# Sum the half chunk of each early pair together with its other sums, and weigh two chunks at a time in the first batch

## The chip, the cores and the metric

One core of one Trainium2 chip. The time is the device time of one execution in microseconds; the kernel before has a median of 624.62 us over three runs (624.58 to 624.62). The names of the engines: PE is the matrix engine, DVE the vector engine, ACT the scalar engine, SP the engine that issues the loads.

## The reference, cut to what matters

Attention for 4 batches of 12 heads (448 queries and keys, 64 values a head), and behind it a two-layer network on the attention's output:

```python
scores = scale * np.matmul(q, k.transpose(0, 1, 3, 2))
scores = cap * np.tanh(scores / cap)
scores = scores - np.max(scores, axis=-1, keepdims=True)
attn = np.exp(scores)
attn = attn / (np.sum(attn, axis=-1, keepdims=True) + 1e-09)
out = np.matmul(attn, v)
h = x @ w_in                      # x: (1792, 768), w_in: (768, 2048)
g = np.where(pos, h, np.where(neg, 0.0, (h + beta) ** 2 / (4.0 * beta)))
y = g @ w_out                     # w_out: (2048, 768)
```

What the change touches is the sum over the keys and the product with v.

## The kernel before, in words

Two heads make a pair; pairs are numbered 0 to 23, six to a batch. Keys stand on the partitions, in four chunks: three of 128 keys, and a last one of 64 keys. In the last chunk both heads of the pair lie in one tile, head 0 on partitions 0 to 63 and head 1 on 64 to 127.

For a chunk c of pair n: `qk` (L362) makes the scores with three float16 products into one of two score tiles `s`; ACT takes the tanh (L370) and the exponential (L372) into a tile `e`; `av` multiplies it with the values `vt` into the one accumulator `av` (L436 for pairs 0 to 11, in float32; L424 for the later pairs, in float16 halves). DVE adds chunks 0 and 1 (L400), and for pairs 6 to 11 chunk 2 as well (L403), into a tile `sums`.

Sums over the partitions are products with a tile of ones into 32 columns, four of them side by side, one for each head and half of the queries, into the tile `t`. For pairs 0 to 11 (`n < HALVED`) the last chunk is summed right behind its own `av` step, with the 64 partitions of each head as they lie (L441); `norm` then adds the product of `sums` (L459), and for pairs 0 to 5 that of chunk 2 too (L459). DVE takes the reciprocal `rr` (L461), ACT or DVE rounds it into the high part of `mix` (L467), DVE makes the low part (L468), a product with `sel` spreads it over the partitions of the two heads (L472, called the spread below), and DVE multiplies the weighted values with it (L481) and splits the product in two float16 tiles `x` (L482, L483).

The network's first layer is L519 to L521, its second L548 to L550: long runs of float16 products, 128 by 128 by 448. Its weights come as 8-byte numbers; DVE turns each piece into two float16 parts in four or five steps (L274, L275, L276, L277 or ACT's L278, L279). DVE also splits queries and keys in two float16 parts (L347 on ACT or DVE, L348 on DVE, tile `spl`). The weights are handled in the first third of the run, while pairs 0 to 11 are computed.

No order is written by hand. Each step is given to a planner with an estimated cost and with the tiles that it reads and writes; the planner runs a list schedule forward and backward five times and takes the best, and each engine then gets its steps in that order. Every step's cost therefore acts on the order of all of them. In a step of `av` the planner counts 105 + 800 ns a chunk, in `norm` 500 + 400 ns for each further chunk.

`tsc` is the factor in front of the tanh (L577, L578); the first tanh waits for it. `qkr` is the tile in which queries and keys land; pair 0's comes in two loads, of 704 and of 256 columns, every other pair's in one of 960.

Of the kernel before, what the change touches and what calls it, by code (L numbers as in the profile page):

```python
# [17 lines left out]
P = 128  # L18
B, H, S, D = 4, 12, 448, 64
NPR = H // 2  # L20
NCK = 4
# [158 lines left out]
def fast_body(ctx, tc, flag, qkp, vp, cap, w_in, w_out, out):  # L180
# [12 lines left out]

    capb, capr, tsc, half = new("capb", [P, 1]), new("capr", [1, 1]), new("tsc", [P, 1]), new("half", [P, 1])
    row = new("row", [1, P])
    ones = new("ones", [P, 32])
    sel, low = new("sel", [P, 2, P], F32R), new("low", [P, 1])
    racc = new("racc", [P, B, 1])
    chk, chr_, okt = new("chk", [P, NCHK]), new("chr", [P, NCHK]), new("okt", [1, NCHK])
# [27 lines left out]
    def take(name, tiles):  # L227

        turn[name] = i = (turn.get(name, -1) + 1) % len(tiles)
        return tiles[i], [("%s%d" % (name, i), None)]  # L230
# [6 lines left out]
    def dve(n, fn, r, w, fast=False):  # L237
        either(r, w, dve_(n, fn, fast))

    def act(n, fn, r, w):  # L240
        either(r, w, act_(n, fn))
# [4 lines left out]
    def pe(cost, fn, r, w):  # L246
        either(r, w, ("PE", cost, fn))
# [142 lines left out]
    def direct(n):  # L390

        return 2 if n < NPR else 3 if n < HALVED else NCK
# [17 lines left out]
    def av(n, cs):  # L410
        if cs[0] == 0:
            st["av", n] = take("av", avs)
        (a, ak), (vt, vk) = st["av", n], st["vt", n]
        if n >= HALVED:
            vh, vk = st["vh", n]

            def run():
                for c in cs:
                    e = st["eh", n, c][0]
                    for x, y in ((0, 0), (0, 1), (1, 0)):  # L420
                        for j in range(2):
                            h = slice(j * D, (j + 1) * D)
                            w, m = (vh[:, x, j * 3 + c], e[:, y, j]) if c < 3 else (vh[h, x, 6], e[h, y, 0])
                            T.matmul(a[h, :S], lhsT=w, rhs=m, start=(c == x == y == 0), stop=(c == 3 and x == 1))  # L424
            pe(105 + 570 * len(cs), run, [k for c in cs for k in st["eh", n, c][1]] + vk + (ak if cs[0] else []), ak)
            return

        t, tk = st["t", n] = take("t", ts) if 3 in cs else (None, [])

        def run():  # L430
            for c in cs:
                e = st["e", n, c][0]
                for j in range(2):
                    h = slice(j * D, (j + 1) * D)
                    w, m = (vt[:, j * 3 + c], e[:, j]) if c < 3 else (vt[h, 6], e[h, 0])
                    T.matmul(a[h, :S], lhsT=w, rhs=m, start=(c == 0), stop=(c == 3))  # L436
                if c == 3:

                    for j, q, half in sums_at():
                        h = slice(j * D, (j + 1) * D)  # L440
                        T.matmul(t[q:q + 32, :S // 2], lhsT=ones[h], rhs=e[h, 0, half], start=True, stop=False, tile_position=(j * D, q))  # L441
        pe(105 + 800 * len(cs), run, [k for c in cs for k in st["e", n, c][1]] + vk + (ak if cs[0] else []) + ([("ones", None)] if tk else []), ak + tk)

    def sums_at():

        return [(j, (1 - j) * D + h * 32, slice(h * S // 2, (h + 1) * S // 2)) for j in range(2) for h in range(2)]

    def norm(n):


        (sm, mk), (a, ak), (t, tk) = st["sums", n], st["av", n], st["t", n] if n < HALVED else take("t", ts)
        (rr, rk), (xf, fk) = take("rr", rrs), take("xf", xfs)
        late = range(direct(n), 3)

        def run():
            for c in [None, *late]:
                for j, q, half in sums_at():
                    m = sm if c is None else st["e", n, c][0]
                    T.matmul(t[q:q + 32, :S // 2], lhsT=ones, rhs=m[:, j, half], start=(n >= HALVED), stop=(c == (late[-1] if late else None)), tile_position=(0, q))  # L459
        pe(500 + 400 * len(late), run, mk + [k for c in late for k in st["e", n, c][1]] + [("ones", None)] + (tk if n < HALVED else []), tk)  # L460
        dve(1340, lambda: V.reciprocal(rr, t[:, :S // 2]), tk, rk)  # L461
        act(S, lambda: A.copy(xf, a[:, :S]), ak, fk)


        (mix, mk) = take("mix", mixs)
        mh, ml = [(mk[0][0], 0)], [(mk[0][0], 1)]
        either(rk, mh, act_(S // 2, lambda: A.copy(mix[:, 0], rr)), dve_(S // 2, lambda: V.tensor_copy(mix[:, 0], rr), True))  # L467
        dve(S // 2, lambda: V.scalar_tensor_tensor(out=mix[:, 1], in0=mix[:, 0].bitcast(F32), scalar=low, in1=rr, op0=ALU.mult, op1=ALU.add), rk + mh + [("sel", None)], ml)  # L468

        def spread():  # L470
            for h in range(2):
                T.matmul(t[:, h * S // 2:(h + 1) * S // 2], lhsT=sel[:, h], rhs=mix[:, 1], start=(h == 0), stop=(h == 1), skip_group_check=True)  # L472
        pe(400, spread, ml + [("sel", None)], tk)
        x, xk = take("x", xs)
        st["x", n] = x, xk[0][0]
        xh, xl = [(xk[0][0], 0)], [(xk[0][0], 1)]
        scale = XS if n < HALVED else 1.0
        if n >= HALVED:
            for j, op in ((CS + n - HALVED, ALU.max), (CS + B * NPR + n - 2 * HALVED, ALU.min)):
                dve(S // 2, lambda j=j, op=op: V.tensor_reduce(out=chk[:, j:j + 1], in_=rr, op=op, axis=AX.X), rk, [("chk", j)])  # L480
        dve(S, lambda: V.scalar_tensor_tensor(out=xf, in0=xf, scalar=scale, in1=t[:, :S], op0=ALU.mult, op1=ALU.mult), tk + fk, fk)  # L481
        either(fk, xh, act_(S, lambda: A.copy(x[:, 0], xf)), dve_(S, lambda: V.tensor_copy(x[:, 0], xf), True))  # L482
        dve(S, lambda: V.tensor_tensor(out=x[:, 1], in0=xf, in1=x[:, 0], op=ALU.subtract), fk + xh, xl)  # L483

    def attention(n):

        split(n)
        if n >= HALVED:
            halve_v(n)
        if n + 2 < B * NPR:  # L490
            load_qk(n + 2)
        for c in range(NCK):
            if n < HALVED:
                qk(n, [c])
            elif c % 2 == 0:
                qk(n, [c, c + 1])
            expo(n, c)
            add(n, c)
            if n >= HALVED:
                halve(n, c)  # L500
            if n < NPR:
                av(n, [c])
            elif c % 2:
                av(n, [c - 1, c])
        if n + 2 < B * NPR:
            load_v(n + 2)
        norm(n)
# [61 lines left out]
            T.matmul(fs[1][:, :S], lhsT=x0[:, :P], rhs=x0, start=True, stop=True)  # L569
    pe(373 * WARM, warm, [("x%d" % (len(xs) - 1), 0)], [("f1", None)])  # L570
    dve(32, lambda: V.memset(ones, 1.0), [], [("ones", None)])
    act(1, lambda: A.activation(half, ones[:, :1], AF.Copy, scale=0.5 * math.sqrt(GS)), [("ones", None)], [("half", None)])
    dve(1, lambda: V.memset(lnes, math.log(ES)), [], [("tsc", 0)])
    dve(P, lambda: V.memset(row, 1.0), [], [("row", None)])
# [511 lines left out]
```

## Time and profile before

| what | value |
|---|---|
| median of 3 runs | 624.62 us |
| profiled execution, its own time | 624.7 us |
| its span | 622.9 us |
| PE busy | 610.5 us (98%) |
| DVE busy | 490.1 us (79%) |
| ACT busy | 402.1 us (65%) |

The span runs from the first to the last instruction. Ends of matmuls are modelled and overlap the next one's start, so the step from one start to the next start tells what a matmul costs. In the views of the time line a row is: start, duration, engine, line, operation, out<-in, shapes, count; what the engine waited for stands in brackets. A matmul in float32 stands as two records. Shapes of PE rows begin with rows*columns of the part of the array that is used: 128*64 is all rows and 64 columns.

### The profile page before, as it was taken

How to read it: one execution, taken by the hardware profiler on the slowest of the kernel's cores; microseconds unless marked ns; L12 is line 12 of the kernel's file. 1: busy time of each engine (PE TensorE's matmuls, PEld its weight loads, DVE VectorE, ACT ScalarE, POOL GpSimd, SP SyncE). 2: the span in 40 equal slices, each digit the busy share in tenths (PEclk: the TensorE clock that was granted, in tenths of full speed). 3: DMA queues.
4: the chain of work that ended last, by engine and by line, in shares of the span. 5: the costliest groups of instructions: out<-in, count | busy, mean ns of one | idle time of the engine just before them, and what ended most of it. 6: DMA issues, size and time to landing. Idle time of an engine off the chain costs nothing.

```text
span 622.9 us, 9197 instructions
## 1 busy us (share of the span) xinstructions
PE 610.5 (98%) x3686; PEld 285.6 (46%) x3686; DVE 490.1 (79%) x674; ACT 402.1 (65%) x587; POOL 0.9 (0%) x5
## 2 busy tenths in 40 slices
PE   7999999999999999999999999999999999999995
PEld 2233455433444444454454444444444555555552
DVE  6999999999999967998886669989975326667452
ACT  6999976899647658898754459989941015451000
POOL 0000000000000000000000000000000000000000
PEclk9999999999999999999999999999999999999999
DMA  8765525235364512423464342215134433337681
GB/s 326 278 237 190 163 69 202 79 119 193 110 250 157 173 41 66 129 65 103 134 207 168 129 149 83 86 63 155 61 133 166 150 128 105 98 93 248 217 290 38
DMA packets 25542, 91.13 MB, mean 146 GB/s; under 512 B 2834, under 2 KB 12178, under 8 KB 22418
## 3 DMA queue, kind: packets, MB, share of 16 engines
q1 hardware_dynamic: 25488, 90.45, 43.3%
q8 instruction: 31, 0.51, 0.3%
q14 instruction: 21, 0.17, 0.1%
q10 hardware_dynamic: 2, 0.00, 0.0%
HBM read 84.93 MB, written 5.51 MB: 145 GB/s over the span
## 4 chain that ended last, share of the span: by engine, by line
PE 82%; ACT 10%; DVE 4%; issue 1%; DMA 1%; SPq 0%; ACTq 0%; DVEq 0%
PE f L548 12%; PE f L549 11%; PE f L550 11%; PE f L519 10%; PE f L520 10%; PE f L521 10%; PE s L362 7%; PE av L424 4%; ACT e L372 4%; ACT e L370 4%; PE av L436 4%; PE t L459 2%; DMA qkr<-qkp 1%; PE t L472 1%; DVE z L381 1%
## 5 line engine op out<-in xcount | busy, mean ns | idle before, releaser
L519 PE MATMUL f<-x,w 128*128 128x448 f16 x384 | 135.6, 353 | 0.8 <-DVE wr L533 0.6
L548 PE MATMUL f<-g,w 128*128 128x448 f16 x384 | 135.5, 353 | 0.0
L549 PE MATMUL f<-g,w 128*128 128x448 f16 x384 | 135.4, 352 | 0.0
L550 PE MATMUL f<-g,w 128*128 128x448 f16 x384 | 135.3, 352 | 0.0
L521 PE MATMUL f<-x,w 128*128 128x448 f16 x384 | 135.3, 352 | 0.0
L520 PE MATMUL f<-x,w 128*128 128x448 f16 x384 | 135.3, 352 | 0.0
L370 ACT ACTIVATE e<-s,tsc 128x896 f32<-128x896 f32 (+1 forms) x96 | 86.0, 903 | 6.9 <-PE s L362 3.9
L290 DVE TENSOR_REDUCE chk<-raw 128x1 f32<-128x768 f32 (+1 forms) x56 | 58.2, 1060 | 23.2 <-DMA raw<-w_out 18.6
L555 ACT ACTIVATE ot<-f 128x448 f32<-128x448 f32 x24 | 13.0, 541 | 85.5 <-PE f L550 85.4
L362 PE MATMUL s<-spl 64*128 64x448 f16 (+1 forms) x504 | 67.0, 352 | 1.1 <-ACT e L370 1.0
L533 DVE SCALAR_TENSOR_TENSOR wr<-f,r 128x448 f32<-128x448 f32 x64 | 39.4, 616 | 26.5 <-ACT r L532 26.3
L531 ACT ACTIVATE r<-f,half 128x448 f32<-128x448 f32 x64 | 40.1, 627 | 24.7 <-PE f L521 24.6
L519 PEld LDWEIGHTS <-w 128*128 128x128 f16 x384 | 37.5, 98 | 39.7 <-issue 6.6
L548 PEld LDWEIGHTS <-w 128*128 128x128 f16 x384 | 37.5, 98 | 37.7 <-issue 4.0
L521 PEld LDWEIGHTS <-w 128*128 128x128 f16 x384 | 37.6, 98 | 35.0
L550 PEld LDWEIGHTS <-w 128*128 128x128 f16 x384 | 37.6, 98 | 34.9
L520 PEld LDWEIGHTS <-w 128*128 128x128 f16 x384 | 37.6, 98 | 34.4 <-issue 1.7
L549 PEld LDWEIGHTS <-w 128*128 128x128 f16 x384 | 37.6, 98 | 34.1 <-DVE w L279 0.5
L372 ACT ACTIVATE e<-e,lnes,capb 128x896 f32<-128x896 f32 (+1 forms) x48 | 49.3, 1038 | 0.9
L536 ACT ACTIVATE g<-wr 128x448 f16<-128x448 f32 x64 | 36.5, 571 | 20.5 <-DVE wr L533 20.4
L372 ACT ACTIVATE e<-e,capb 128x896 f32<-128x896 f32 (+1 forms) x48 | 45.4, 949 | 1.2
L436 PE MATMUL av<-e,vt 128*64 128x448 f32 (+1 forms) x192 | 44.1, 559 | 1.7 <-ACT e L372 1.6
(80 smaller groups left out, 732.4 us busy)
## 6 DMA issues: line engine op xcount, KB each, us to landing
qkr<-qkp SPq DMA_DIRECT2D x47, 480.0 KB, 3.7
raw<-w_out SPq DMA_DIRECT2D x17, 1024.0 KB, 4.8
raw<-w_in SPq DMA_DIRECT2D x18, 768.0 KB, 4.3
vt<-vp SPq DMA_DIRECT2D x48, 224.0 KB, 3.1
w<-w_in SPq DMA_DIRECT2D x14, 768.0 KB, 6.6
w<-w_out SPq DMA_DIRECT2D x7, 1024.0 KB, 5.0
out<-ot SPq DMA_DIRECT2D x24, 224.0 KB, 2.0
qkr<-qkp SPq DMA_DIRECT2D x1, 352.0 KB, 3.1
```

What stands on the lines that cost most here:

```text
L290: dve(width, lambda j=j, op=op: V.tensor_reduce(out=chk[:, j:j + 1], in_=hi, op=op, axis=AX.X, apply_absolute_value=True), rk + after, [(" ...
L362: T.matmul(s[:, j, :S], lhsT=t[h, a, S + c * P:S + (c + 1) * P], rhs=t[h, b, :S], start=(i == 0), stop=(i == 2))
L370: act(w * S + 60, lambda: A.activation(e[:, :w], s[:, :w, :S], AF.Tanh, scale=tsc), sk + [("tsc", None)], ek)
L372: act(w * S + 110, lambda: A.activation(e[:, :w], e[:, :w], AF.Exp, scale=capb, **bias), ek + [("tsc", None)], ek)
L436: T.matmul(a[h, :S], lhsT=w, rhs=m, start=(c == 0), stop=(c == 3))
L519: T.matmul(ph, lhsT=w1[:, 0, fc, c], rhs=x[c][0][:, 0], start=(c == 0), stop=False)
L520: T.matmul(ph, lhsT=w1[:, 1, fc, c], rhs=x[c][0][:, 0], start=False, stop=False)
L521: T.matmul(ph, lhsT=w1[:, 0, fc, c], rhs=x[c][0][:, 1], start=False, stop=(c == NCC - 1))
L531: act(S + (170 if acc else 0), lambda: A.activation(r, ph, AF.Relu, bias=half, scale=0.5 * root / (WS * XS), **acc), fk + [("half", None)] ...
L548: T.matmul(po, lhsT=hi[:, fc], rhs=gv[:, 0], start=(fc == 0), stop=False)
L549: T.matmul(po, lhsT=lo[:, fc], rhs=gv[:, 0], start=False, stop=False)
L550: T.matmul(po, lhsT=hi[:, fc], rhs=gv[:, 1], start=False, stop=(fc == NFC - 1))
```

## The change

- Pairs 0 to 11: the last chunk is no longer summed behind its `av` step. `norm` now sums it in the same run as `sums` and chunk 2, over all 128 partitions, with a new tile `halves` in place of ones: its first 32 columns are one on the first 64 partitions and zero on the others, its last 32 columns the other way round.
- Pairs 0 to 5: `av` takes chunks 0 and 1 in one step and 2 and 3 in one, as the later pairs did already.
- Three small fills of `halves` on DVE at the start.

```diff
-    ones = new("ones", [P, 32])
+    ones, halves = new("ones", [P, 32]), new("halves", [P, 2, 32])
...
-                if c == 3:
-
-                    for j, q, half in sums_at():
-                        h = slice(j * D, (j + 1) * D)
-                        T.matmul(t[q:q + 32, :S // 2], lhsT=ones[h], rhs=e[h, 0, half], start=True, stop=False, tile_position=(j * D, q))
...
-        late = range(direct(n), 3)
+        late = range(direct(n), NCK)
...
-                    T.matmul(t[q:q + 32, :S // 2], lhsT=ones, rhs=m[:, j, half], start=(n >= HALVED), stop=(c == (late[-1] if late else None)), tile_position=(0, q))
-        pe(500 + 400 * len(late), run, mk + [k for c in late for k in st["e", n, c][1]] + [("ones", None)] + (tk if n < HALVED else []), tk)
+                    w, m = (ones, m[:, j, half]) if c != 3 else (halves[:, j], m[:, 0, half])
+                    T.matmul(t[q:q + 32, :S // 2], lhsT=w, rhs=m, start=(c is None), stop=(c == (late[-1] if late else None)), tile_position=(0, q))
+        pe(500 + 400 * len(late), run, mk + [k for c in late for k in st["e", n, c][1]] + [("ones", None), ("halves", None)], tk)
...
-            if n < NPR:
-                av(n, [c])
-            elif c % 2:
+            if c % 2:
                 av(n, [c - 1, c])
...
+    dve(64, lambda: V.memset(halves, 0.0), [], [("halves", None)])
+    for j in range(2):
+        dve(32, lambda j=j: V.memset(halves[j * D:(j + 1) * D, j], 1.0), [], [("halves", None)])
```

Lines behind `av` have other numbers after the change: L436 is L435, L459 is L454, L461 is L456, L468 is L463, L472 is L467, L481 is L476, L483 is L478, L533 is L526, L537 is L530, L577 is L573. The number at the end of a name counts the tiles; `halves` makes it one higher for most.

PE, pair 0's last chunk and its sums, before:

```order
L362 MATMUL s_139<-spl_91 128x448
L436 MATMUL av_142<-e_97,vt_92 64x448 x2
L441 MATMUL t_143<-e_97,ones 32x224 x4
L459 MATMUL t_143<-sums_103,ones 32x224 x4
L459 MATMUL t_143<-e_96,ones 32x224 x4
L362 LDWEIGHTS spl_91
```

And after:

```order
L362 MATMUL s_140<-spl_92 128x448
L454 MATMUL t_144<-sums_104,ones 32x224 x4
L454 MATMUL t_144<-e_97,ones 32x224 x4
L454 MATMUL t_144<-e_98,halves 32x224 x4
L435 MATMUL av_143<-e_97,vt_93 64x448 x2
L435 MATMUL av_143<-e_98,vt_93 64x448 x2
L362 LDWEIGHTS spl_92
```

All three sums now stand in one run, ahead of the last two chunks' products with the values.

DVE at the start (the first pairs' splits and the factor of the tanh), before:

```order
L348 SCALAR_TENSOR_TENSOR spl_90<-qkr_88,spl_90 128x704
L348 SCALAR_TENSOR_TENSOR spl_90<-qkr_88,spl_90 128x256
L577 RECIPROCAL tsc<-t_143 128x1
L578 TENSOR_SCALAR tsc<-tsc 128x1
L579 TENSOR_SCALAR capb<-t_143 128x1
L348 SCALAR_TENSOR_TENSOR spl_91<-qkr_89,spl_91 128x960
L274 TENSOR_SCALAR z_86<-w_0_79 128x768
```

And after:

```order
L348 SCALAR_TENSOR_TENSOR spl_91<-qkr_89,spl_91 128x704
L348 SCALAR_TENSOR_TENSOR spl_91<-qkr_89,spl_91 128x256
L348 SCALAR_TENSOR_TENSOR spl_92<-qkr_90,spl_92 128x960
L573 RECIPROCAL tsc<-t_144 128x1
L574 TENSOR_SCALAR tsc<-tsc 128x1
L575 TENSOR_SCALAR capb<-t_144 128x1
L274 TENSOR_SCALAR z_87<-w_0_80 128x768
```

The factor of the tanh now stands behind pair 1's split. On ACT pair 0's 256 columns are split ahead of pair 1's 960 now (DVE did it before), and SP issues pair 1's load ahead of pair 0's 256 columns.

DVE ahead of pair 10's reciprocal (the last row), before:

```order
L348 SCALAR_TENSOR_TENSOR spl_91<-qkr_89,spl_91 128x960
L400 TENSOR_TENSOR sums_103<-e_94,e_95 128x896
L481 SCALAR_TENSOR_TENSOR xf_132<-xf_132,t_143 128x448
L483 TENSOR_TENSOR x_106<-xf_131,x_106 128x448
L403 TENSOR_TENSOR sums_103<-sums_103,e_96 128x896
L275 SCALAR_TENSOR_TENSOR z_86<-raw,z_86 128x1024
L533 SCALAR_TENSOR_TENSOR wr_135<-f_140,r_133 128x448
L276 SCALAR_TENSOR_TENSOR z_86<-raw,z_86 128x1024
L461 RECIPROCAL rr_129<-t_143 128x224
```

And after:

```order
L276 SCALAR_TENSOR_TENSOR z_87<-raw,z_87 128x1024
L275 SCALAR_TENSOR_TENSOR z_88<-w_5_85,z_88 128x1024
L478 TENSOR_TENSOR x_107<-xf_132,x_107 128x448
L276 SCALAR_TENSOR_TENSOR z_88<-w_5_85,z_88 128x1024
L400 TENSOR_TENSOR sums_104<-e_95,e_96 128x896
L476 SCALAR_TENSOR_TENSOR xf_133<-xf_133,t_144 128x448
L403 TENSOR_TENSOR sums_104<-sums_104,e_97 128x896
L526 SCALAR_TENSOR_TENSOR wr_137<-f_142,r_135 128x448
L296 TENSOR_REDUCE chk<-x_111 128x1
L348 SCALAR_TENSOR_TENSOR spl_91<-qkr_89,spl_91 128x960
L456 RECIPROCAL rr_130<-t_144 128x224
```

By this reciprocal one more piece of weights has gone through DVE after the change (the piece in `w_5` is under way, which before was begun behind it), and one more split.

## Rows read from the trace of the kernel before

**Rows 1.** Stretches of core 0: busy time and count of each engine.

```profile
18.00:61.80 43.80, 43.32 (x333) 14.63 (x331) 41.56 (x56) 42.33 (x56) 0.00 (x0) 1.00 0.64 232
61.80:115.00 53.20, 53.20 (x303) 25.88 (x300) 51.79 (x73) 43.13 (x68) 0.00 (x0) 1.00 0.39 129
115.00:162.50 47.50, 46.17 (x313) 16.47 (x310) 45.99 (x58) 46.72 (x67) 0.00 (x0) 1.00 0.40 133
```

**Rows 2.** What PE waited for, 0 to 163 us: total, times, longest.

```profile
PE av L436 <- ACT e L372: 1.6, 5, 0.4
PE t L472 <- DVE mix L468: 1.0, 2, 0.6
```

**Rows 3.** What DVE waited for, 0 to 163 us.

```profile
DVE rr L461 <- PE t L459: 2.1, 4, 1.1
DVE w L279 <- ACT w L278: 0.8, 2, 0.5
```

**Rows 4.** Time line of PE, pair 0's last chunk and its sums.

```profile
14.93 0.74 PE L362 MATMUL s<-spl 64*128 64x448 f16 x6
15.60 0.97 PE L436 MATMUL av<-e,vt 64*64 64x448 f32 x4
16.50 0.58 PE L441 MATMUL t<-e,ones 64*32 64x224 f32 x8
17.01 0.59 PE L459 MATMUL t<-sums,ones 128*32 128x224 f32 x8
17.41 0.56 PE L459 MATMUL t<-e,ones 128*32 128x224 f32 x8
17.91 0.74 PE L362 MATMUL s<-spl 64*128 64x448 f16 x6
```

**Rows 5.** Time line of PE: an av run of two chunks; one set of sums alone.

```profile
27.85 1.72 PE L436 MATMUL av<-e,vt 128*64 128x448 f32 x8
29.51 0.74 PE L362 MATMUL s<-spl 64*128 64x448 f16 x6
...
149.90 0.59 PE L459 MATMUL t<-sums,ones 128*32 128x224 f32 x8
150.42 1.60 PE L362 MATMUL s<-spl 64*128 64x448 f16 x9
```

**Rows 6.** Time line of DVE at the start.

```profile
6.80 0.17 DVE L577 RECIPROCAL tsc<-t 128x1 f32<-128x1 f32 x1 [0.92 <-PE t L576]
8.09 1.16 DVE L348 SCALAR_TENSOR_TENSOR spl<-qkr,spl 128x960 f16<-128x960 f32 x1 [0.86 <-ACT spl L347]
10.25 0.56 DVE L274 TENSOR_SCALAR z<-w 128x768 int32<-128x768 int32 x1 [1.00 <-DMA w<-w_in]
```

**Rows 7.** Time line of ACT at the start.

```profile
7.05 1.00 ACT L347 ACTIVATE spl<-qkr 128x960 f16<-128x960 f32 x1 [2.43 <-DMA qkr<-qkp]
7.96 0.99 ACT L370 ACTIVATE e<-s,tsc 128x896 f32<-128x896 f32 x1
```

**Rows 8.** Time line of DVE around the reciprocals of pairs 10 and 11.

```profile
150.64 1.55 DVE L461 RECIPROCAL rr<-t 128x224 f32<-128x224 f32 x1
...
158.29 0.69 DVE L274 TENSOR_SCALAR z<-w 128x1024 int32<-128x1024 int32 x1
158.89 1.55 DVE L461 RECIPROCAL rr<-t 128x224 f32<-128x224 f32 x1
160.35 0.56 DVE L537 SCALAR_TENSOR_TENSOR g<-wr,g 128x448 f16<-128x448 f32 x1
160.83 1.21 DVE L275 SCALAR_TENSOR_TENSOR z<-w,z 128x1024 int32<-128x1024 int32 x1
161.96 0.44 DVE L468 SCALAR_TENSOR_TENSOR mix<-mix,low,rr 128x224 fp32r<-128x224 f32 x1
```

**Rows 9.** Time line of PE: the spreads of pairs 10 and 11, and the last products.

```profile
154.01 0.48 PE L472 MATMUL t<-mix,sel 128*128 128x224 f32 x2 [0.34 <-DVE mix L468]
162.46 0.48 PE L472 MATMUL t<-mix,sel 128*128 128x224 f32 x2 [0.61 <-DVE mix L468]
...
616.13 0.35 PE L549 MATMUL f<-g,w 128*128 128x448 f16 x1
616.32 0.35 PE L550 MATMUL f<-g,w 128*128 128x448 f16 x1
```

More of the change, by code (lines that the diff above doesn't have):

```diff
@@ L426, in av @@
             return
-        t, tk = st["t", n] = take("t", ts) if 3 in cs else (None, [])
         def run():
@@ L436, in run @@
                     T.matmul(a[h, :S], lhsT=w, rhs=m, start=(c == 0), stop=(c == 3))
-                if c == 3:
-                    for j, q, half in sums_at():
-                        h = slice(j * D, (j + 1) * D)
-                        T.matmul(t[q:q + 32, :S // 2], lhsT=ones[h], rhs=e[h, 0, half], start=True, stop=False, tile_position=(j * D, q))
-        pe(105 + 800 * len(cs), run, [k for c in cs for k in st["e", n, c][1]] + vk + (ak if cs[0] else []) + ([("ones", None)] if tk else []), ak + tk)
+        pe(105 + 800 * len(cs), run, [k for c in cs for k in st["e", n, c][1]] + vk + (ak if cs[0] else []), ak)
     def sums_at():
@@ L448, in norm @@
     def norm(n):
-        (sm, mk), (a, ak), (t, tk) = st["sums", n], st["av", n], st["t", n] if n < HALVED else take("t", ts)
+        (sm, mk), (a, ak), (t, tk) = st["sums", n], st["av", n], take("t", ts)
         (rr, rk), (xf, fk) = take("rr", rrs), take("xf", xfs)
-        late = range(direct(n), 3)
+        late = range(direct(n), NCK)
         def run():
```

## The prediction

> **What bounds the kernel now.** I read the stretches first, then the waits of PE and DVE, then the time line where they meet. In the stretches from 18 to 162.5 us, where pairs 0 to 11 are computed and the weights are taken apart, the reader should see that no engine has room: PE is busy for 142.7 of 144.5 us, DVE for 139.3, ACT for 132.2 [rows 1]. A busy PE alone would not say that PE is the bound, but the waits do: it waited for ACT 1.6 us in five places and for DVE 1.0 us at two spreads [rows 2]. So PE leads here, and DVE follows with 5.2 us of idle time. Part of that idle time is PE's doing: four reciprocals waited 2.1 us for the sums [rows 3]. At pair 11 DVE is the late one already: its reciprocal starts at 158.89, though PE was done with the sums, and the spread behind it keeps PE waiting until 162.46 [rows 8, 9]. From there PE runs nearly without a gap to its last product at 616.32 [rows 9].
>
> **The change part by part.** *PE, the sums.* Each change of the array's shape costs PE time, and that is what the change removes. One set of sums alone takes 0.52 us (149.90 to 150.42), two sets in a row 0.90 (17.01 to 17.91), so one more set of the same shape costs 0.38 [rows 4, 5]. The old set of the last chunk, in a shape of its own, took 0.51 (16.50 to 17.01) [rows 4]. Moved, it costs 0.13 less, and in twelve pairs that is 1.6 us. The zeros in `halves` cost nothing that these rows show: both shapes stream 224 columns for four products side by side.
>
> The Trainium skill (TensorEngine Tiling (Array Packing), Restrictions and Gotchas, Gotcha 1) says that different row tiles must not use one PSUM bank at the same time. The old sums do just that, two heads on different rows into `t`; by that rule they would have run one head after the other, some 0.8 us a set, and the change would give back about 4 us more. The trace does not agree: 0.51 us for the whole set [rows 4].
>
> *PE, two chunks a step.* One chunk of `av` takes 0.90 us up to the next shape (15.60 to 16.50), two take 1.66 (27.85 to 29.51), so a merged step saves 0.15 and the scores around it about 0.1 more [rows 4, 5]. But the planner had merged many of them already: along PE's order the runs of full chunks fall from 25 to 23 only. All in all PE's order has 255 changes of shape before and 241 after. At the 0.10 to 0.15 us that each pair of neighbours costs on the time line, they come to 25.0 and 22.4 us: 2.6 us less, 2.3 of it ahead of pair 11's spread and 0.3 behind. If PE alone set the time, this would be the gain.
>
> *The start.* The order puts the factor of the tanh behind pair 1's split on DVE. Before it was ready at about 7.2 us and the first tanh started at 7.96, when ACT was through with pair 1's split [rows 6, 7]. After, ACT has 256 columns more in front (at 1.00 us for 960, about 0.3 us) and starts pair 1's split when that load has landed, between 6.2 and 7.05 us; it ends at 7.4 to 8.3. DVE's low part takes 1.16 more, the factor 0.4, so the first tanh starts at 9.0 to 9.9: 1.0 to 1.9 us late. I take 1.5. The trace of before can't show how much of it stays. Its cover is DVE: DVE starts on the weights when their load lands, at 10.25, both times [rows 6], and by pair 5 ACT has about 1.7 us less to do, since the order gives some of it to later pairs. So I take nothing for it as long as DVE sets the time, and 1.5 if that cover is gone.
>
> The Trainium skill (TensorE: Matmul & The Clock Gate, the table at its beginning) calls DVE's and ACT's queues strictly first in, first out, with eight entries. That speaks against this change: the factor can't overtake the split. The trace agrees as far as it goes, since all of DVE's instructions start in the program's order; if they could overtake, the 1.5 us would be nothing.
>
> *DVE, ahead of pairs 10 and 11.* The change takes nothing off DVE, but the new order moves work forward. Counted along the order, pair 10's reciprocal has ahead of it, more than before: one step each of L274, L275, L276 and L279 on 1024 columns (0.60 and three times 1.13 from start to start), a split in both parts (1.07 and 0.57), and two steps of 0.53, less a rounding of 0.30 that ACT takes: 6.4 us [rows 8]. The split's low part is the 1.16 of the start less 0.09 by which DVE's rows overlap [rows 6]; the last ones are estimated from rows of the same width. Pair 11's reciprocal has the same 6.4 us ahead of it.
>
> **The sum.** It is made at pair 11's spread, since PE has all attention of pairs 0 to 11 ahead of it in both orders. Behind it PE has less to do after the change: 1971 products of the network instead of 1995, at 0.19 us each (616.13 to 616.32) 4.55 us, and 0.3 for fewer shapes; 4.85 in all. So the end moves by (new spread - 162.46 - 4.85) [rows 9]. Say DVE saves s us of its idle time on the way.
>
> By DVE: pair 11's reciprocal comes at 158.89 + 6.4 - s. From it to the spread it was 3.57 us with L537 and L275 between; L274 stands there too now, 0.60, so 4.2 [rows 8, 9]. The spread comes at 169.5 - s.
>
> By PE: pair 10's reciprocal comes at 150.64 + 6.4 - s, its spread 3.5 us later (3.37 before, and a copy of 0.15) [rows 8, 9]. From that spread to the next PE has pair 11's first step of `av`, six products of the network, two sets of sums, the second step of `av` and 21 products, with their changes of shape 9.9 us at the prices above. The spread comes at 170.4 - s.
>
> The later of the two counts: 170.4 - s, and the end moves by 3.1 - s. For s, zero is one end; the other is about 4.6, all of DVE's 5.2 us but what it waits for ACT (0.8 of it at L279 [rows 3]). I take 2.6: the 2.1 us in which reciprocals waited for PE go, since DVE is now the one behind, and 0.5 of the rest. That gives +0.5 us. The profiled execution took 624.7 us, 0.08 more than the median; on the median that is 625.1 us. So the 2.6 us that PE saves turn into waits at the spreads of pairs 6 to 11. This last part of the forecast has its own range, 623.4 to 625.9.
>
> **The rivals.** *PE keeps the lead.* If DVE runs with hardly any idle time (s of 4.4 or more), PE's savings come through: up to 2.6 us, 622.0. For it: DVE has 5.2 us to give. Against it: DVE, ACT and PE all hang on each other here, and a chain of three full engines does not run without gaps. With s at 4.4 it begins to count as faster, 623.4.
>
> *DVE keeps its idle time.* The same 6.4 us of weights and splits stand ahead of pair 10's reciprocal, but DVE still waits for loads, roundings on ACT and exponentials as before (s under 1.8). PE then stands at the spreads of pairs 10 and 11 for 3 to 5 us in all, and the end moves by +1.3 to +3.1: 625.9 to 627.7. For it: PE waited for these two spreads before [rows 2, 9]. Against it: part of the idle time was PE's doing.
>
> *The start stays.* ACT, which is 97% busy from 18 to 61.8 us [rows 1], never wins back the late tanh; then reciprocals of pairs 2 to 5 come 1.5 us late, DVE waits for them, and the end moves by 0.5 + 1.5 = 2.0 us: 626.6. Against it: the 1.7 us that ACT has less to do by pair 5.
>
> **How the numbers follow.** The forecast, no change that can be told, has 0.42. PE keeps the lead: 0.24. DVE keeps its idle time: 0.24. The start stays: 0.10. A change under 0.2% (1.25 us) can't be told from none here, so faster is 0.24, same 0.42, slower 0.34. The stretch behind pair 11, where the planner has moved work too, adds about 1 us either way, which no row here settles. Left out below is the end of the faster case and above that of the slowest, a tenth each: 622.4 to 627.6.
>
> **What would show it.** In the profile after: no PE row with 64*32; three sets of sums in a row, 1.27 us up to the next shape; the first tanh at 9.0 to 9.9 us; PE waiting for DVE at L467 for 3 us or more between 60 and 170 us, against 1.0 before; pair 11's spread at about 167.8. If that spread starts before 166 us with PE's waits no longer than before, DVE was not the bound and the forecast is wrong on the fast side; if PE waits over 5 us there, on the slow side. If the first tanh stands at 8 us, my reading of the start is wrong.

## The result, and the profile after

The changed kernel takes 627.0 us (median of eight runs, 626.35 to 631.21), the kernel before 624.62 (eight runs beside them): a ratio of 1.0052, 95% interval 1.0037 to 1.0066. It is slower by 2.4 us, where I forecast no change (625.1). The profiled execution took 627.01 us, its span is 625.1. Single runs are longer the lower the granted clock: 626.35 at a mean of 0.999, 631.21 at 0.992.

The stretches that answer to [rows 1], with the start ahead of them (us; busy time and count of PE, PEld, DVE, ACT, POOL; PE's granted clock; DMA share; GB/s):

```profile
9.00:12.00 3.00, 1.39 (x9) 0.51 (x8) 2.46 (x4) 2.93 (x4) 0.00 (x0) 0.99 1.02 418
12.00:15.30 3.30, 3.30 (x11) 0.88 (x12) 3.30 (x6) 3.23 (x5) 0.00 (x0) 0.50 1.01 419
...
18.00:61.80 43.80, 43.59 (x339) 15.65 (x337) 43.34 (x59) 41.49 (x57) 0.00 (x0) 1.00 0.67 242
61.80:115.00 53.20, 51.34 (x291) 24.85 (x288) 52.22 (x74) 42.13 (x65) 0.00 (x0) 1.00 0.35 118
115.00:162.50 47.50, 46.71 (x317) 17.48 (x318) 44.44 (x55) 46.20 (x64) 0.00 (x0) 1.00 0.46 161
```

Two stretches are new. PE is busy for 1.39 of 3.00 us from 9 to 12 us (2.39 before, at a clock of 1.00 there and behind it), and then works at half its clock. And from 61.8 to 115 us, where it was busy all of 53.20 us before, it has 1.9 us of idle time.

What PE waited for, up to 163 us (answers to [rows 2]):

```profile
PE s L362 <- ACT e L370: 4.5, 4, 1.9
PE f L562 <- DVE x L558: 2.0, 1, 2.0
PE t L467 <- DVE mix L463: 0.7, 1, 0.7
PE f L512 <- DVE wr L526: 0.5, 1, 0.5
```

The waits at the spreads (L467), which I had put at 3 us or more, are 0.7. In their place PE waits 4.5 us at the scores until the tanh has read the score tile out, 3.1 of it at the start. (L562 is the warm-up, outside the forecast.) That kind of wait was there before as well, in one place, a row that the prediction left out when it read PE's waits for ACT:

```profile
PE s L362 <- ACT e L370: 1.0, 1, 1.0
```

DVE's waits for the sums have gone from 2.1 to 0.9, in the direction forecast, but a wait for exponentials has come (answers to [rows 3]):

```profile
DVE sums L400 <- ACT e L372: 2.0, 2, 1.3
...
DVE rr L456 <- PE t L454: 0.9, 2, 0.6
```

Behind 163 us, PE's one wait, before and after:

```profile
PE f L519 <- DVE wr L533: 0.6, 2, 0.3
```

```profile
PE f L512 <- DVE wr L526: 2.2, 3, 1.0
```

The start, on the time line (answers to [rows 4, 6, 7]):

```profile
5.46 1.31 ACT L347 ACTIVATE spl<-qkr 128x256 f16<-128x256 f32 x2 [0.87 <-DMA qkr<-qkp]
...
6.80 1.16 DVE L348 SCALAR_TENSOR_TENSOR spl<-qkr,spl 128x960 f16<-128x960 f32 x1 [0.47 <-ACT spl L347]
7.88 0.16 DVE L573 RECIPROCAL tsc<-t 128x1 f32<-128x1 f32 x1
8.32 1.01 ACT L370 ACTIVATE e<-s,tsc 128x896 f32<-128x896 f32 x1 [1.56 <-DVE capb L575]
9.38 0.74 PE L362 MATMUL s<-spl 64*128 64x448 f16 x6 [1.86 <-ACT e L370]
...
11.35 0.73 PE L362 MATMUL s<-spl 128*128 128x448 f16 x3 [1.22 <-ACT e L370]
...
12.01 3.26 PE L435 MATMUL av<-e,vt 128*64 128x448 f32 x8
...
16.50 0.59 PE L454 MATMUL t<-sums,ones 128*32 128x224 f32 x8
...
16.90 0.56 PE L454 MATMUL t<-e,ones 128*32 128x224 f32 x8
...
17.28 0.56 PE L454 MATMUL t<-e,halves 128*32 128x224 f32 x8
```

The factor stands behind pair 1's split, and ACT waits 1.56 us for it and the bound computed with it; PE then waits twice for ACT. The weighted values at 12.01 took 3.26 us at half the clock; the same group took 1.72 in [rows 5]. The sums' last set is in the new shape.

The reciprocals and spreads of pairs 10 and 11 and the last product (answer to [rows 8, 9]):

```profile
154.27 1.55 DVE L456 RECIPROCAL rr<-t 128x224 f32<-128x224 f32 x1
...
164.07 1.55 DVE L456 RECIPROCAL rr<-t 128x224 f32<-128x224 f32 x1
```

```profile
158.64 0.37 PE L467 MATMUL t<-mix,sel 128*128 128x224 f32 x1
...
168.44 0.35 PE L543 MATMUL f<-g,w 128*128 128x448 f16 x1
168.47 0.43 PE L467 MATMUL t<-mix,sel 128*128 128x224 f32 x1
...
618.74 0.35 PE L543 MATMUL f<-g,w 128*128 128x448 f16 x1
```

The last product starts 2.42 us later than before. By the sum's own rule the spread accounts for 168.47 - 162.46 - 4.85 = 1.16 of it; the stretch behind the spread, 450.27 us instead of the 449.01 that the rule expects (453.86 before, less 4.85), for 1.26.

### The profile page after: what moved, and what is told of

Same layout as the page of the kernel before. It is cut to its first block, busy times and chain, and to the rows that moved or that the text cites. A ratio compares the mean times of both kernels' runs of the same rounds, so it can differ in the third digit from the quotient of the medians.

```text
span 625.1 us, 9185 instructions
## 1 busy us (share of the span) xinstructions
PE 608.9 (97%) x3686; PEld 287.0 (46%) x3686; DVE 490.0 (78%) x676; ACT 401.3 (64%) x588; POOL 0.9 (0%) x5
## 4 chain that ended last, share of the span: by engine, by line
PE 70%; ACT 16%; DVE 11%; issue 2%; DMA 1%; SPq 0%; ACTq 0%; DVEq 0%
PE f L541 12%; PE f L542 11%; PE f L543 11%; PE f L512 7%; PE f L513 6%; PE f L514 6%; PE s L362 6%; ACT e L370 5%; ACT e L372 5%; PE av L424 4%; PE av L435 4%; PE t L454 2%; DVE wr L526 2%; ACT r L525 1%; DVE g L530 1%
## 5 line engine op out<-in xcount | busy, mean ns | idle before, releaser
L526 DVE SCALAR_TENSOR_TENSOR wr<-f,r 128x448 f32<-128x448 f32 x64 | 39.8, 621 | 19.5 <-ACT r L525 18.9
L530 DVE SCALAR_TENSOR_TENSOR g<-wr,g 128x448 f16<-128x448 f32 x64 | 39.4, 619 | 6.6 <-ACT g L529 5.7
```

Source lines behind the costliest of these rows:

```text
L526: dve(S, lambda: V.scalar_tensor_tensor(out=w, in0=ph, scalar=WS * XS, in1=r, op0=ALU.max, op1=ALU.min), fk + rk, wk)
L530: dve(S, lambda: V.scalar_tensor_tensor(out=t[:, 1], in0=w, scalar=down, in1=t[:, 0], op0=ALU.mult, op1=ALU.subtract), wk + [(gk, 0)], [(g ...
```

## The experiments

Each is timed beside the kernel before, on one chip; the chips differ from run to run. The starts (us) of the spreads of pairs 0, 5, 6, 11 and of the last product in each profile locate a gain, where two kernels have one order:

| kernel | median us | ratio to before, 95% | spread 0 | 5 | 6 | 11 | last product |
|---|---|---|---|---|---|---|---|
| before | 624.6 | 1 | 21.73 | 65.49 | 114.30 | 162.46 | 616.32 |
| changed | 627.0 | 1.0052 [1.0037, 1.0066] | 20.90 | 62.26 | 113.52 | 168.47 | 618.74 |
| e1 | 624.1 | 0.9987 [0.9978, 0.9996] | 21.46 | 64.93 | 113.61 | 161.75 | 615.59 |
| e6 | 628.09 | 1.0050 [1.0037, 1.0063] | 20.85 | 62.75 | 114.12 | 169.20 | 619.48 |
| e8 | 623.67 | 0.9983 [0.9974, 0.9992] | 22.79 | 64.86 | 109.70 | 167.33 | 615.25 |
| e10 | 623.66 | 0.9989 [0.9981, 0.9998] | 22.72 | 64.65 | 109.38 | 166.88 | 614.91 |
| e4 | 627.06 | 1.0046 [1.0029, 1.0063] | 20.21 | 61.58 | 112.83 | 167.76 | 618.02 |
| e5 | 627.15 | 1.0039 [1.0026, 1.0052] | 20.52 | 61.91 | 113.16 | 168.12 | 618.40 |
| e14 | 626.97 | 1.0031 [1.0020, 1.0043] | 21.44 | 62.80 | 114.05 | 169.03 | 620.03 |
| e15 | 627.04 | 1.0034 [1.0024, 1.0045] | 20.38 | 61.74 | 113.00 | 167.96 | 618.25 |
| e16 | 624.33 | 0.9998 [0.9989, 1.0007] | 21.37 | 65.10 | 113.91 | 161.75 | 615.59 |
| e17 | 626.44 | 1.0031 [1.0019, 1.0044] | 21.20 | 62.56 | 113.07 | 167.79 | 618.09 |
| e18 | 626.29 | 1.0024 [1.0013, 1.0035] | 20.86 | 62.23 | 112.75 | 167.47 | 617.77 |
| e19 | 626.15 | 1.0029 [1.0016, 1.0042] | 20.20 | 61.30 | 112.56 | 167.51 | 617.78 |

e1, e16 have before's order; e10 has e8's; e4 to e6 and e14 to e19 (but e16) have the changed kernel's, but for the steps moved or added.

Each place comes from one profile, and two things scatter in it. The first tanh starts at 8.22 to 8.88 us in the eight profiles of the changed order with nothing moved ahead of it, so the places carry some tenths of a us of the start; differences between two places of one profile don't. And a profiled run's time is 8.0 to 9.7 us more than the start of its last product, from kernel to kernel without a pattern, so medians of few runs are coarser than the places.

### What the new shape is worth by itself

e1: the kernel before, its order kept; only the last chunk's sums take the new shape.

```diff
-            for c in [None, *late]:
+            for c in [None, *late, *([3] if n < HALVED else [])]:
...
+                    w, m = (ones, m[:, j, half]) if c != 3 else (halves[:, j], m[:, 0, half])
```

> The order of all engines is the kernel before's, step for step; only the last chunk of pairs 0 to 11 is summed with the masked ones, in one run with the other sums, and the masked ones are filled in the step that fills the ones. So the shapes of the array change 12 times less (243 changes instead of 255) and nothing else moves. Theory A (PE leads in that order, and what the change lost it lost by the new order): PE gives back 0.13 us a pair, 1.6 us in all, and the time falls to about 623.0 us (622.8 to 623.6). Theory B (PE, ACT and DVE are all full in this stretch, so PE's savings drown in waits whatever the order): 624.2 to 624.8 us, with PE waiting 1 to 1.6 us more for ACT and DVE between 14 and 163 us.

e6: the changed kernel, its order kept; those sums in their old shape.

```diff
-                    w, m = (ones, m[:, j, half]) if c != 3 else (halves[:, j], m[:, 0, half])
+                    h = slice(j * D, (j + 1) * D)
+                    w, m = (ones, m[:, j, half]) if c != 3 else (ones[h], m[h, 0, half])
...
-        ... tile_position=(0, q))
+        ... tile_position=(0 if c != 3 else j * D, q))
```

> The changed kernel's order word for word, but the last chunk's sums in their old shape (64 rows of ones per head, 64*32), at their new place behind the other sets. 254 runs of one shape on PE instead of 242. If PE leads in this order too, the old shape costs 12 x 0.13 = 1.6 us: 628.6. If PE waits anyway (the theory: the saving is eaten by about 1 us of waits), 0.6 us: 627.6. If PE's savings are worth nothing in this order: 627.0.

In before's order the new shape brings the last product 0.73 us forward, in the changed order 0.74 (619.48 - 618.74); counted from PE's first score it is 0.68 and 0.84. e1's interval lies below 1, while e6's and the changed kernel's overlap. Neither time fell into a range that I had given: e1's 624.10 lies between Theory A and Theory B, e6's 628.09 between the counts with 0.6 and with 1.6 us. So the shape is a gain of about 0.7 us, less than half of the 12 x 0.13 = 1.6 that I counted. And e6, which has the old shape, still ends 619.48 - 616.32 = 3.2 us behind the kernel before (2.3 to 3.9 by the interval of its times): that is what the new order costs, with the sums' new place and the steps of two chunks in it, and that is the case.

### What other orders bring

e8: the kernel before, only the planner told of the set's cost. e10: e8's order with e1's shape.

```diff
-        pe(105 + 800 * len(cs), run, ...
+        pe(105 + 800 * len(cs) + (400 if tk else 0), run, ...
```

> The kernel before, instruction for instruction, with one number of the planner changed: the step with the last chunk of pairs 0 to 11 is given 400 ns more, for the sums that it holds and that the planner did not count. Only the order moves. Theory A (the order is what costs; a planner that counts PE's sums packs the other engines' work differently, and a new order is worth one or two us either way): a time clearly apart from 624.6, by my guess slower, 625.5 to 628. Theory B (an order that counts rightly is better): 622.5 to 624. Theory C (orders of this planner are all alike): 624.3 to 625.0.

> The order of the kernel before as the planner makes it when it counts 400 ns for the last chunk's sums (623.67 us by itself), with those sums in the new shape (64*32 becomes 128*32, no shape of their own). Theory (a new order moves the time through short waits, and the shape's saving is partly eaten by waits, 0.6 us in the order of the kernel before): about 623.0 us, between 622.4 and 623.5. Rival (PE's saving comes through in full, 12 x 0.13): 622.1. Rival (any saving of PE's turns into waits): 623.7.

e9 and e13: the changed kernel's steps, the planner counting 0 or 200 ns for the last chunk's set in place of 400.

```diff
-        pe(500 + 400 * len(late), run, mk ...
+        pe(500 + 400 * (len(late) - (n < HALVED)), run, mk ...              # e9
+        pe(500 + 400 * len(late) - (200 if n < HALVED else 0), run, mk ...  # e13
```

> The changed kernel with all its steps; only the planner's cost of the step with the sums leaves the last chunk's set out (100 + 400 per other set less, as the kernel before had it), so that only the order is another. Theory (it is the order that the planner found which costs 2.4 us, by waits at the start, at 62 to 92 us and behind pair 11): another order has other waits, between 624 and 627 us, and the waits of PE for the tanh at 62.9 us need not be there. Rival (the steps cost by themselves: two chunks at a time come late, three sets in a row hold PE up): 627 again.

> The changed kernel, the planner counting 200 ns instead of 400 for the last chunk's set; same steps, another order (the changed kernel 627.0 with 400, 625.04 with 0). Theory (each order is a draw, the price has no trend): anywhere from 623.5 to 627.5. Rival (counting the set pushes work behind it smoothly): midway, 626.0.

e2 is the first part alone, e3 the second; e12 is e10 with the second part.

```diff
-            if c % 2:                  # e2, against the changed kernel
+            if n < NPR:
+                av(n, [c])
+            elif c % 2:
...
-            if n < NPR:                # e3 against before, e12 against e10
-                av(n, [c])
-            elif c % 2:
+            if c % 2:
```

> The first part alone: sums of the last chunk in the new shape and place, weighted values chunk by chunk as before, the planner's own order. 251 runs of one shape on PE instead of 256 before and 242 after. If the sums' part carries the cost: 626 to 627 us. If the steps of two chunks carry it: 624 or less. Theory (the order found each time decides, not a part): either, with waits of PE in other places than after's 62.9 us.

> The second part alone: the first batch's weighted values in steps of two chunks, the last chunk's sums in their old shape and place, the planner's own order. 255 runs of one shape on PE, one less than before. Theory (the order found decides, not a part): within 1.5 us of the kernel before, 623.0 to 626, and the difference is PE's idle time, as its places in the profile show. Rival (steps of two chunks make PE wait for the second chunk's exponential): 626 or more, with PE waiting at L435.

> Both parts of the change's idea without moving the sums in the planner's list: sums of the last chunk in the new shape, but t taken and 400 ns counted in the step of the weighted values as in the faster order (623.66 us without this edit), and that step of two chunks. A new order once more. Theory (the order decides): between 622.5 and 626, its distance from 623.66 equal to the difference in PE's idle time and shape changes. Rival (two chunks a step save 0.1 to 0.25 us each and are always a gain): 623.0 or less.

A number that changes no instruction moved the kernel before to 623.67 us (e8, faster, against what I expected) and the changed kernel to 625.04 (e9, 1.0010 [0.9998, 1.0022]) and 624.53 (e13, 1.0001 [0.9993, 1.0010]). Prices of 0, 200 and 400 ns give 625.0, 624.5 and 627.0: no trend, so the rival of a smooth push falls. e2 came to 626.54 (1.0036 [1.0023, 1.0049]), e3 to 625.11 (1.0017 [1.0002, 1.0032]), e12 to 627.03 (1.0052 [1.0033, 1.0071]). e2's time is the one that I had named for the case that the sums' part carries the cost. But e13 has both parts, step for step as the changed kernel, and stands level with before, so the steps don't force the loss: the order does. Two chunks a step are not always a gain either: the same edit on e10 cost 3.4 us, more than either side of that forecast allowed. e10 adds next to nothing to e8 (last product 0.34 us earlier, medians alike), as the last rival there had it.

### What in this order costs: the start

e4 puts pair 0's first chunk of weighted values, for which all is ready, into PE's wait; e5 puts 13 products there whose result nobody reads, and e11 does so in e9.

```diff
+            if n == 0 and cs == [2]:             # e4, in the step of the scores
+                st["early"]()                    # av of chunk 0, taken out of the step [0, 1]
...
+            if n == 0 and cs[0] in (1, 2):       # e5, e11
+                for _ in range((0, 8, 5)[cs[0]]):
+                    T.matmul(fs[1][:, :S], lhsT=x0[:, :P], rhs=x0, start=True, stop=True)
```

> The changed kernel in its own order, with one thing undone: pair 0's first chunk is multiplied with its values right behind the scores of chunk 2, as in the kernel before, and no longer together with chunk 1. Theory A (the wait at the start starves PE, its clock falls to 1.2 GHz for some us, and this is what scatters the changed kernel's times): the granted clock stays at full from the first score on, PE's step with chunks 0 and 1 no longer takes 3.2 us, the runs lie within 1 us of each other, and the median falls by 0.5 to 1.5 us, to 625.5 to 626.5. What is left over the kernel before (1 to 1.8 us) is the order behind. Theory B (the start explains everything): 624.6 or below. Theory C (the scatter has another cause): runs from 626.3 to over 629 as before.

> The changed kernel in its own order, with 13 more products of zeros on PE in the two gaps of the start (8 behind the scores of chunk 1, 5 behind those of chunk 2, into a bank that nothing uses yet): PE does more and is idle less, and nothing else moves. Theory A (idle PE lets the clock fall): no stretch at half clock before the end, the scatter goes, the median is that of the changed kernel's undisturbed runs, 626.3 to 626.7 us. Theory C (the clock falls for another reason): the scatter stays, 626.3 to 631 us.

> The changed kernel with the order found when the planner leaves the last chunk's set out of its cost (625.04 us, single runs from 623.4 to 627.6 with a granted clock from 0.997 down to 0.992), and 13 products of zero's value to nobody (8 and 5) in PE's two waits for the first tanhs, as in the changed kernel with a filled start. Theory (PE's waits at the start let the granted clock fall in part of the runs, and that is the scatter): runs within 1 us of each other, about 624.0. Rival (the scatter comes from the waits at 60 to 66 us, where this order's profile shows the clock at half level from 64.6 to 68.0): scatter as before, 625.0.

The medians stayed at 627, against the forecasts of a gain. e4's runs scatter as before (626.44 to 629.90), though its one profile shows no fall of the clock at the start. But e5's five runs lie within 626.58 to 627.46, where the changed kernel's go to 631.21, and so do those of e15 and e18 below, which have the same filling (626.45 to 627.50 and 625.50 to 627.44). So filling the start takes the long runs away; the median it hardly moves. e11 took away e9's longest runs (623.77 to 626.36 instead of 623.39 to 627.63) but not a group some 2 us above the lowest, and its median is 625.16 (1.0009 [0.9999, 1.0019]), the rival's. e9's profile shows the fall at 64.6 us:

```profile
56.00:64.60 8.60, 6.98 (x62) 3.14 (x61) 8.38 (x12) 7.42 (x11) 0.00 (x0) 1.00 0.53 173
64.60:68.00 3.40, 3.40 (x11) 0.79 (x9) 3.26 (x6) 3.40 (x5) 0.00 (x0) 0.50 0.18 33
```

In e5 spread 0 came 0.38 us earlier, and spreads 5, 6, 11 and the last product 0.35, 0.36, 0.35 and 0.34: the order is rigid, and what the start gives is kept to the last product. The 0.38 is not an earlier tanh's doing, for e5's came 0.21 us later. From the first tanh to spread 0 it takes 12.0 us in the profiles of e4, e5, e15 and e18, and 12.6 in those of the changed kernel, e14 and e17, in which the clock fell at the start: such a fall costs 0.6 us. So e19 takes away what the forecast named there. Three steps on DVE are moved in the finished order:

```diff
+        todo, k = plan.order(), st["tsc"]        # k, k + 1, k + 2: factor and bound, L573 to L575
+        p = [j for j, (i, e) in enumerate(todo) if e == "DVE" and todo.index((k, "DVE")) > j][-1]
+        moved = [x for x in todo if x[0] in (k, k + 1, k + 2)]
+        todo = [x for x in todo[:p] if x not in moved] + moved + [x for x in todo[p:] if x not in moved]
```

> The changed kernel's order with three steps of VectorE moved by hand: the factor of the tanh and the bound (L573 to L575) ahead of the low part of pair 1's split, which stands in front of them in this order and behind them in the kernel before. Nothing else moves. The first tanh starts at about 7.0 us instead of 8.32. Theory (in this order the start is on the path: with the filled start every later spread and the last product stood 0.34 to 0.38 us earlier, as the first spread did): spread 0, spread 11 and the last product 0.7 to 1.3 us earlier, median 625.7 to 626.3. Rival (a later wait takes the gain, as with the moved scores): 627.

```profile
6.66 0.17 DVE L574 RECIPROCAL tsc<-t 128x1 f32<-128x1 f32 x1 [0.38 <-PE t L572]
...
7.34 1.01 ACT L370 ACTIVATE e<-s,tsc 128x896 f32<-128x896 f32 x1 [0.63 <-PE s L362]
8.40 0.74 PE L362 MATMUL s<-spl 64*128 64x448 f16 x6 [0.53 <-ACT e L370]
```

The first tanh starts at 7.34 instead of 8.32; spread 0 stands 0.70 us earlier, spread 5, spread 11 and the last product all 0.96. The median is 626.15, the lowest run 625.33 against 626.35. These are the theory's numbers, but they are not the factor's alone. The clock did not fall in e19's profile and did in the changed kernel's; against e4 and e5, where it did not fall either, e19's last product is only 0.24 and 0.62 us earlier, and PE now waits 0.95 us for DVE at spread 0. And e19's interval overlaps those of the changed kernel, e4 and e5. So the late factor, with the clock's fall in the waits behind it, is worth up to 0.9 us; the factor alone, by these profiles, 0.2 to 0.6.

### What in this order costs: the scores of pair 6

The longest wait of PE behind the start is 1.22 us at 64.83, pair 6's last scores. e14 moves that one step behind the 18 products and the weighted values that follow; e15 does it in e5.

```diff
+        todo, late = plan.order(), st["at", 6, 3]
+        p = [i for i, _ in todo].index(late)
+        step, q = todo.pop(p), p
+        for _ in range(3):
+            q = next(j for j in range(q, len(todo)) if todo[j][1] == "PE") + 1
+        todo.insert(q, step)
```

> The changed kernel's order with one step moved by hand: pair 6's scores of the last chunk, for which PE waits 1.22 us at 64.83 us for the tanh to read their buffer out, are put behind the next 18 products of the network and the next step of weighted values, so that PE has work while it waited. Nothing else moves; 242 runs of one shape as before. Theory (idle time of PE in this order is lost time, since PE leads): spread 6 and the last product 1.2 us earlier, 625.8 us. Rival (the network's products then wait for DVE's bound at 80 to 92 us instead, where PE already stands 0.9 us): last product unmoved, 627.0.

> The same move together with the 13 products that fill PE's waits at the start (627.15 us by themselves, no scatter). Theory: 627.15 less 1.2, 625.9. Rival: 627.1.

```profile
62.35 0.74 PE L362 MATMUL s<-spl 64*128 64x448 f16 x6
63.02 0.36 PE L516 MATMUL f<-x,w 128*128 128x448 f16 x1
...
64.77 0.35 PE L516 MATMUL f<-x,w 128*128 128x448 f16 x1 [0.44 <-ACT x L481]
...
67.41 1.72 PE L439 MATMUL av<-e,vt 128*64 128x448 f32 x8
69.07 1.41 PE L362 MATMUL s<-spl 128*128 128x448 f16 x9
```

In e15 (above, PE) the wait at the scores is gone, but the products in its place wait for `x` from ACT, and from spread 0 to spread 6 it takes 92.62 us in the changed kernel, 92.61 in e14, 92.64 in e5 and 92.62 in e15. Nothing is won: the rival, though its place was wrong (64.8 us, not 80 to 92). (e14's last product stands later still, by a wait of 0.56 us for ACT at 212.93 that only its profile has.)

### What in this order costs: DVE's work

In the changed kernel the chain that ended last runs over ACT and DVE from 62 to 115 us, where it ran over PE in the kernel before (first row before, second the changed kernel, cut at its end):

```profile
by line: PE f L519 28.2%; PE f L520 27.9%; PE f L521 27.8%; PE s L362 6.7%; PE av L436 6.5%; PE t L472 1.2%; PE t L459 1.0%; PE t L441 1.0%
```

```profile
by line: ACT e L372 12.9%; ACT e L370 11.4%; DVE z L276 10.0%; DVE wr L526 9.4%; DVE z L275 8.4%; DVE g L530 8.4%; DVE w L279 8.4%; DVE z L274 6.4%; issue 6.0%; ACT w L278 4.2%; ACT r L525 3.3%; ACT r L524 3.2%; DVE rr L456 2.8%; DVE sums L
```

e16 (of before), e17 (of the changed kernel) and e18 (of e5) relieve DVE, orders kept. I had counted 18 x 0.87 = 15.7 us; the profiles show 16 such pieces, the last at 110 us in e16 and 105 in e17, not 165, each 0.95 us long and now 0.15, and DVE's busy time falls by 10.8 us in e16 and 10.9 in e17.

```diff
+        n = 1 if k < 0 else width
-        dve(width, lambda: V.scalar_tensor_tensor(out=zb, in0=lo, scalar=29, in1=zb, ...
+        dve(width, lambda: V.scalar_tensor_tensor(out=zb[:, :n], in0=lo[:, :n], scalar=29, in1=zb[:, :n], ...
```

> The kernel before in its own order, VectorE relieved: L275, which puts the last 3 bits into each piece of the first weights, runs on 1 column instead of 768 in all 18 pieces (these bits are left out); 18 times 0.87 us, 15.7 us of VectorE's work ahead of pair 11's spread, at 20 to 165 us. The chain of waits of this kernel is TensorE's from 62 to 115 us, so VectorE's relief should bring little: the 1.0 us of waits at two spreads and some of what hangs on the reciprocals, 623.5 us (622.5 to 624.6).

> The changed kernel in its own order, VectorE relieved in the same way. Theory (the time that TensorE saves is lost because VectorE, with ScalarE, sets the pace from 62 to 170 us in this order): the relief gives back far more than in the kernel before, 2.5 to 4 us, and the changed kernel comes level with the kernel before so relieved or below, 623 to 624.5 us. Rival (TensorE's waits come from ScalarE's exponentials, from the start and from the order of the network's products, not from VectorE): the same gain as in the kernel before, some 626 us, 2 us above it.

> The changed kernel with its filled start (627.15 us), VectorE relieved in the same way, so that the granted clock's scatter doesn't hide the answer. Theory: 623 to 624.3 us. Rival: 626.

The chain of e17 in the same stretch:

```profile
by line: PE f L513 25.2%; PE f L515 24.6%; PE f L514 24.6%; ACT e L371 7.2%; PE av L436 6.5%; ACT e L373 5.9%; PE s L363 4.3%; PE t L455 1.7%; issue 0.3%
```

DVE is off the chain, and still it brought little. From spread 0 to the last product e17 needs 596.89 us against 597.84, e18 596.91 against 597.88: 0.95 and 0.97 us. e16 needs 594.22 against 594.59: 0.37. So by this relief DVE holds 0.6 us of the difference between the orders, not 2, and 2.1 us (1.0031 against 0.9998) stay with DVE relieved in both. The theory that DVE sets the pace from 62 to 170 us falls as far as the relief reaches; the rival's 626 came, and e16's 624.33 lay in its range. Of DVE behind 105 us these runs say little, and no run relieved ACT, for whose tanh PE waits longest.

## Why the prediction was wrong, step by step

- *The sums.* The three sets take 1.27 us, as forecast. But "12 x 0.13 = 1.6 us" was mis-sized as a gain of the kernel: 0.73 us in one order, 0.74 in the other (e1, e6). PE's busy time between its first score and its last product does fall by 1.4 and 1.25 us there, but its idle time grows by 0.7 and 0.4.
- *The start.* The order was read rightly, the factor behind pair 1's split. The first tanh came at 8.32 us, not 9.0 to 9.9, because pair 1's load had landed earlier and ACT split it from 5.78 on, right behind the 256 columns: 0.36 us later than before, not 1.0 to 1.9. "I take nothing for it" failed even so: DVE did wait for the load of the weights, until 9.47 us, but that covered nothing, since a shift of spread 0 was kept to the last product (e4, e5), and up to 0.9 us came back when the tanh was moved (e19). The rival "the start stays", which I gave 0.10, had this step right, though not its size, nor the fall of PE's clock that came with it.
- *DVE ahead of pairs 10 and 11.* The step that failed is "the 2.6 us that PE saves turn into waits at the spreads of pairs 6 to 11". With s at 2.6 the reciprocals were to come at 154.4 and 162.7 and the spread at 167.8; they came at 154.27, 164.07 and 168.47. The numbers are near, the reason isn't: PE waited 0.7 us at the spreads, not 3, and it reaches pair 11's spread out of a run of products without a gap (168.44, then 168.47). Taking 10.9 us of work off DVE brought 0.95 us. I took the engine whose count I could make along the order for the one that sets the time. The rival "DVE keeps its idle time" has 627.0 in its range, 625.9 to 627.7, by luck: at pair 11's reciprocal s was 1.2, as it asks, but PE did not stand 3 to 5 us at the two spreads.
- *Behind pair 11.* The sum held nothing for the "about 1 us either way, which no row here settles"; it came out as +1.26. PE waits for DVE to read the network's tiles out, 2.2 us instead of 0.6. At the longest of these places DVE has attention's work ahead of `wr`:

```profile
262.41 1.08 DVE L381 TENSOR_TENSOR eh<-e,eh 128x896 f16<-128x896 f32 x1
263.50 0.62 DVE L408 TENSOR_TENSOR sums<-sums,e 64x448 f32<-64x448 f32 x1
264.15 0.62 DVE L526 SCALAR_TENSOR_TENSOR wr<-f,r 128x448 f32<-128x448 f32 x1
```

```profile
263.44 0.35 PE L514 MATMUL f<-x,w 128*128 128x448 f16 x1
264.83 0.35 PE L512 MATMUL f<-x,w 128*128 128x448 f16 x1 [1.04 <-DVE wr L526]
```

  e5, e17, e18 and e19 all keep this gap; no run took it away, so that its 1.26 us are the loss is read, not shown.

What makes up the 2.42 us can be read from PE's busy time between its first score and its last product (kernel before, then the changed one):

```profile
6.70:18.00 11.30, 9.32 (x76) 2.90 (x77) 9.23 (x14) 10.78 (x13) 0.00 (x0) 1.00 0.99 393
18.00:163.00 145.00, 143.19 (x946) 57.36 (x945) 139.84 (x185) 132.67 (x190) 0.00 (x0) 1.00 0.47 161
163.00:616.32 453.32, 452.56 (x2655) 223.16 (x2653) 338.05 (x458) 255.83 (x383) 0.73 (x1) 1.00 0.41 136
```

```profile
6.22:18.00 11.78, 8.70 (x68) 3.26 (x69) 9.45 (x16) 9.59 (x11) 0.00 (x0) 0.86 0.96 379
18.00:163.00 145.00, 142.14 (x947) 58.13 (x945) 140.34 (x185) 130.32 (x186) 0.00 (x0) 1.00 0.48 169
163.00:618.74 455.74, 453.54 (x2661) 223.79 (x2660) 337.24 (x457) 257.78 (x388) 0.72 (x1) 1.00 0.39 133
```

PE stands idle 1.98, 1.81 and 0.76 us before, and 3.08, 2.86 and 2.20 after: 3.6 us more. Its busy time falls by 0.7 us, although 3.3 us of it ran at half clock; taking half of those 3.3 off, an estimate, PE has 2.3 us less to do. So the forecast's 2.6 us of saved work came nearly whole. What failed is where they would go: the 3.6 us of waits and the 1.65 us of the clock outweigh them, and the first score came 0.5 us earlier (3.6 + 1.65 - 2.3 - 0.5 = 2.4).

That says where PE stood, not what each wait would give back. The runs show that for a part only: up to 0.9 us at the start (e19), 0.6 for DVE's load up to some 105 us (e16, e17), nothing for the scores' wait at 64.8 us (e14, e15). For the waits behind 163 us it is not shown, nor whether these parts overlap.

## What to carry to other kernels

Where a planner sets the order, every edit also draws a new order, and here a draw alone, by a number that changes no instruction, moved the median by 1.0 us (e8 against the kernel before) and 2.5 us (e13 against the changed kernel), more than the 0.7 us of the new shape: forecast it as a term with its own spread, and measure an edit with the order kept (e1, e6) and the order without the edit (e8). A wait, or an engine on the chain that ended last, is not yet a price: the 1.2 us wait at the scores cost nothing, and DVE, with more than half of the chain from 62 to 115 us, gave less than 1 us for 10.9 us of work. A shift of the first spread was kept to 0.04 us by 600 us of work (e4, e5, e15); look there first. e8, e10 and e1 beat both kernels, by about 0.1 to 0.2% (0.9983, 0.9989 and 0.9987, intervals below 1).

## What the runs showed of the hardware

PE's clock fell to 1.2 GHz from 12.0 to 15.3 us after a stretch in which PE worked 1.39 of 3.00 us (changed kernel), and in e9 from 64.6 to 68.0 after 6.98 of 8.60; in the changed kernel the group of weighted values that it met took 3.26 us instead of 1.72, and by spread 0 the fall had cost 0.6 us. How long the clock is down differs from run to run of one program: e3's runs go from 623.57 us at a mean clock of 0.997 to 628.00 at 0.991. With products that nobody reads in the waits of the start, the clock stayed up there in all four profiles (e5, e11, e15, e18), and the medians show no cost (e5 against the changed kernel).

Old sums of two heads, on different rows of the array and into one tile, ran side by side: the whole set took 0.51 us [rows 4], as much as a set over all rows alone, 0.52 [rows 5].
